# Grouped-query attention with a KV cache: the last two rows of wo re-cut, row 31 in two column halves and row 30 in loads of 120 and 8 partitions

## The chip, the cores and the metric

The kernel runs on one core of a Trainium2 chip. The metric is the device time of one execution in microseconds; lower is better. The kernel before took 363.76 us (median of three runs, 363.58 to 363.94). "Span" is the part of an execution that the profile covers; it is some 1.8 us shorter than the device time. PE is the matrix engine, ACT and DVE are the engines that here cast and copy results, SP is the sequencer that issues the loads (SPq in the views), PEld is PE's loading of weights, and 16 DMA engines move the data. The granted clock is the share of PE's full clock that it had; it was 0.995 to 1.0 in every execution but one (0.99).

## The reference

Shortened:

```python
# B, Sq, D = 32, 4, 1024; Hq, Hkv, Sk, Dh = 32, 4, 2048, 128; all bf16
def reference(x, k_cache, v_cache, wq, wo):
    q = (x @ wq).reshape(B, Sq, Hq, Dh).transpose(0, 2, 1, 3)
    k = jnp.repeat(k_cache, rep, axis=1)          # rep = Hq // Hkv = 8
    v = jnp.repeat(v_cache, rep, axis=1)
    scores = jnp.einsum("bhqd,bhkd->bhqk", q, k) * (Dh ** -0.5)
    p = softmax(scores, axis=-1)
    o = jnp.einsum("bhqk,bhkd->bhqd", p, v)
    return o.transpose(0, 2, 1, 3).reshape(B, Sq, Hq * Dh) @ wo
```

The K and V caches are 134 MB of the 151 MB that are read. wo has 4096 x 1024 elements; the kernel reads it as 32 "rows" (the code's `u` or `h`), each a 128 x 1024 tile of 256 KB, with one matmul contraction of 128 for each row and half of the columns.

## The kernel before: the parts that matter here

SP issues all the loads in one queue: x, wq, then K and V batch by batch, and wo last, into K and V buffers that have come free. The list `WO` says how many rows go into each wo load. The code below is cut out of the kernel; `# ...` marks what is left out.

```python
WO = (4, 4, 4, 4, 4, 4, 2, 2, 2, 1, 1)
# ...
            return big[:, wo_slot[u // 8], :, :].rearrange("p t d -> p (t d)")[:, u % 8 * D:(u % 8 + m) * D]

        wo_v = wo.rearrange("(h p e) n -> p h (e n)", p=128, e=4)
        u0 = 0
        for c, m in enumerate(WO):
            assert u0 // 4 == (u0 + m - 1) // 4
            kind, b = wo_for[u0 // 8]
            dst, src = wo_at(u0, m), wo_v[:, u0 // 4, u0 % 4 * D:(u0 % 4 + m) * D]
            p.dma("sp", lambda e, dst=dst, src=src: e.dma_start(dst, src),
                [("kt", b, 1) if kind == "k" else ("pv", b)], ("wo", c), f"s_wo{c}")
            u0 += m
        assert u0 == Hq
```

The output projection takes the rows in order. Each row is two matmuls of 512 columns, which add to two halves of a PSUM tensor over all rows; a row's matmuls wait for the semaphore of the load that holds the row. Then ACT and DVE cast a half each, and two DMAs write the result.

```python
        def oproj(c):
            for h in range(sum(WO[:c]), sum(WO[:c + 1])):
                for j in range(2):
                    out_, lhsT, rhs = ps_s[:, NC * j:NC * (j + 1)], oT_of(h), wo_at(h, 1)[:, NC * j:NC * (j + 1)]
                    if j == 0:
                        mm = lambda e, a=(out_, lhsT, rhs), h=h: e.matmul(
                            a[0], lhsT=a[1], rhs=a[2], start=(h == 0), stop=(h == Hq - 1), skip_group_check=True)
                    else:
                        mm = lambda e, a=(out_, lhsT, rhs), h=h: _matmul_held(
                            nc, e, *a, tile_size=(128, 128), tile_position=(0, 0), start=(h == 0), stop=(h == Hq - 1))
                    p.op("pe", mm, [("wo", c), ("ot", B - 1)], ("op", j) if h == Hq - 1 else None)

        def oproj_out():
            p.op("act", lambda e: e.activation(y_sb[:, 0:NC], ps_s[:, 0:NC], ACT.Copy), [("op", 0)], ("oe", 0))
            p.op("dve", lambda e: e.tensor_copy(y_sb[:, NC:D], ps_s[:, NC:D]), [("op", 1)], ("oe", 1))
            for j, eng in enumerate(("act", "sp")):
                p.dma(eng, lambda e, j=j: e.dma_start(out_flat[:, NC * j:NC * (j + 1)], y_sb[:, NC * j:NC * (j + 1)]),
                      [("oe", j)], ("out", j), f"s_o{j}")
```

## Time and profile before

| | before |
|---|---|
| device time, median | 363.76 us |
| span of the profiled run | 361.8 us |
| DMA engines | full at about 430 GB/s from the second slice of 40 to the last but one |
| last K or V load complete | 338.15 us |
| rows 28 and 29 (one load) complete | 356.86 us |
| row 30 complete | 357.50 us |
| row 31 complete | 358.13 us |
| last matmul starts | 358.43 us |
| end of the span | 361.8 us |

Two kinds of record are read in this document. The views of the profile (page, chain of waits, timeline, windows) show instructions and waits. Below them, the trace has two lists that no view prints: the time of each semaphore increment by which a DMA engine reports its share of a load, and the start, the duration and the size of each DMA packet. Numbers from these lists stand in plain fences or tables. A load of 128 partitions reports 16 increments; it is complete with the 16th. The packet list has them as packets of 4 bytes: 1296 for the 81 DMAs that SP issues in the kernel before, 16 each. That kernel's packets of the loads from 353 us on chain into 16 strings, each start within 8 ns of the end before it; where a string can be followed, eight packets of a load come before one of 4 bytes. A packet here is one contiguous run: 8 KB for four rows, 4 KB for two, 2 KB for one, 1 KB for half a row.

### The profile page before, as it was taken

How to read it: one execution, taken by the hardware profiler on the slowest of the kernel's cores; microseconds unless marked ns; L12 is line 12 of the kernel's file. 1: busy time of each engine (PE TensorE's matmuls, PEld its weight loads, DVE VectorE, ACT ScalarE, POOL GpSimd, SP SyncE). 2: the span in 40 equal slices, each digit the busy share in tenths (PEclk: the TensorE clock that was granted, in tenths of full speed). 3: DMA queues.
4: the chain of work that ended last, by engine and by line, in shares of the span. 5: the costliest groups of instructions: out<-in, count | busy, mean ns of one | idle time of the engine just before them, and what ended most of it. 6: DMA issues, size and time to landing. Idle time of an engine off the chain costs nothing. (4 is left out here: it accounts for less than half of the span.)

```text
span 361.8 us, 6213 instructions
## 1 busy us (share of the span) xinstructions
PE 307.2 (85%) x3002; PEld 146.8 (41%) x2338; DVE 269.1 (74%) x170; ACT 102.8 (28%) x110; POOL 165.3 (46%) x262
## 2 busy tenths in 40 slices
PE   1988788999989999988999888888888889889896
PEld 1002000454444554444444444444333344449711
DVE  0018799999899888879998888888888888856500
ACT  1014222333333333333333333333322223333000
POOL 8002055355555555554455444445555554444000
PEclk9999999999999999999999999999999999999999
DMA  8999999999999999999999999999999999999995
GB/s 322 431 435 429 431 426 424 431 428 426 423 426 431 426 433 424 430 427 429 431 422 433 428 429 422 431 429 427 431 422 433 429 429 426 427 433 429 408 417 195
DMA packets 11819, 151.66 MB, mean 419 GB/s; under 512 B 1312, under 2 KB 1568, under 8 KB 2336
## 3 DMA queue, kind: packets, MB, share of 16 engines
q1 hardware_dynamic: 11664, 151.39, 98.7%
q8 instruction: 6, 0.10, 0.1%
q10 hardware_dynamic: 144, 0.13, 0.1%
q14 instruction: 5, 0.04, 0.0%
HBM read 151.26 MB, written 0.26 MB: 419 GB/s over the span
## 5 line engine op out<-in xcount | busy, mean ns | idle before, releaser
L325 DVE STREAM_TRANSPOSE KT_sb<-big 128x2048 f32<-128x2048 f32 x64 | 146.6, 2293 | 16.7 <-DMA big<-in_k_cache_dram 16.7
L351 ACT ACTIVATE P_sb<-ps_s,negmx 128x2048 bf16<-128x2048 f32 x32 | 82.1, 2565 | 185.0 <-DVE negmx L347 185.0
L16 PE MATMUL ps_s<-KT_sb,QD_sb 128*128 128x512 bf16 x384 | 103.7, 377 | 0.0
L382 POOL COPY PD_sb<-PT_sb 32x1024 f32<-32x1024 f32 x62 | 64.1, 1034 | 63.4 <-PE ps_r L391 60.5
L382 POOL COPY big<-PT_sb 32x1024 f32<-32x1024 f32 x61 | 63.0, 1034 | 59.1 <-PE ps_r L391 56.4
L347 DVE TENSOR_REDUCE negmx<-ps_s 128x1 f32<-128x2048 f32 x32 | 73.2, 2287 | 12.4 <-PE ps_s L16 11.0
L391 PE MATMUL ps_r<-big 128*128 128x128 bf16 x1024 | 59.8, 219 | 11.3 <-PEq L85 11.3
L391 PE MATMUL ps_r<-big,PD_sb 128*128 128x128 bf16 x1024 | 59.8, 219 | 9.9 <-PEq L85 9.9
L391 PEld LDWEIGHTS ps_r<-big 128*128 128x128 bf16 x1024 | 57.9, 98 | 22.1 <-issue 21.6
L391 PEld LDWEIGHTS ps_r<-big,PD_sb 128*128 128x128 bf16 x1024 | 58.0, 98 | 21.1 <-issue 20.6
L338 PE MATMUL ps_s<-KT_sb,QD_sb 128*128 128x512 bf16 x128 | 48.3, 377 | 18.4 <-PEq L85 18.4
L338 PEld LDWEIGHTS ps_s<-KT_sb,QD_sb 128*128 128x128 bf16 x128 | 12.4, 97 | 103.1 <-issue 103.1
L360 DVE STREAM_TRANSPOSE PT_sb<-P_sb 128x1024 f32<-128x1024 f32 x32 | 39.8, 1245 | 15.8 <-ACT P_sb L351 15.8
L315 POOL COPY QD_sb<-QT_sb 32x64 f32<-32x64 f32 x128 | 29.4, 229 | 46.2 <-DVE QT_sb L294 20.5
L16 PE MATMUL ps_r<-ident 128*128 128x384 bf16 x173 | 33.3, 325 | 0.0
L363 PEld LDWEIGHTS ps_r<-ssum,permf 128*128 128x128 f32 x64 | 11.9, 187 | 24.8 <-issue 23.1
L400 ACT ACTIVATE QT_sb<-ps_r,rinv 128x128 bf16<-128x128 f32 x32 | 11.7, 367 | 29.5 <-PE ps_r L391 27.3
L276 DVE TENSOR_SCALAR KT_sb<-ps_r 128x512 bf16<-128x512 f32 x2 | 1.3, 686 | 20.2 <-PE ps_r L260 20.2
L417 PE MATMUL ps_s<-big,KT_sb 128*128 128x512 bf16 x32 | 12.2, 380 | 2.2 <-DMA big<-in_wo_dram 1.4
L426 DVE CAST P_sb<-ps_s 128x512 bf16<-128x512 f32 x1 | 0.7, 692 | 16.1 <-PE ps_s L16 16.1
L16 PE MATMUL ps_s<-big,KT_sb 128*128 128x512 bf16 x32 | 12.1, 379 | 0.0
L249 PE MATMUL ps_r<-ident 128*128 128x384 bf16 x32 | 10.3, 323 | 0.0
(41 smaller groups left out, 85.1 us busy)
## 6 DMA issues: line engine op xcount, KB each, us to landing
big<-in_k_cache_dram SPq DMA_DIRECT2D x32, 2048.0 KB, 18.6
big<-in_v_cache_dram SPq DMA_DIRECT2D x32, 2048.0 KB, 22.0
big<-in_wq_dram SPq DMA_DIRECT2D x4, 2048.0 KB, 14.1
big<-in_wo_dram SPq DMA_DIRECT2D x6, 1024.0 KB, 22.8
big<-in_wo_dram SPq DMA_DIRECT2D x3, 512.0 KB, 24.5
big<-in_wo_dram SPq DMA_DIRECT2D x2, 256.0 KB, 21.0
P_sb<-in_x_dram SPq DMA_DIRECT2D x1, 256.0 KB, 2.7
out_dram<-P_sb ACTq DMA_DIRECT2D x1, 128.0 KB, 1.8
```

Source lines behind the costliest of these rows:

```text
L16: return eng.add_instruction(mybir.InstMatmult(name=nc.get_next_instruction_name(), engine=eng.engine, start_tensor_calc=start, stop_tenso ...
L315: p.op("pool", lambda e, s=src, d=dst: e.tensor_copy(d, s), waits if g == 0 else [("pt", i - 2)] * (g == 1 and i > 1), ("qd", i) if g == G ...
L325: p.op("dve", lambda e, s=src, d=dst: e.transpose(d, s), waits, ("kt", i, c), gives="t_kt" if c else None)
L338: mm = lambda e, a_=(out_, lhsT, rhs), f=first, l=last: e.matmul(a_[0], lhsT=a_[1], rhs=a_[2], start=f, stop=l, skip_group_check=True)
L347: p.op("dve", lambda e: e.tensor_reduce(negmx[:, i % 4:i % 4 + 1], ps_s[:, :], AX.X, ALU.max, negate=True), [("qk", i)], ("negmx", i))
L351: p.op("act", lambda e: e.activation(P_sb[:, :, :, :].rearrange("p t r w -> p t w r"), ps_s[:, :].rearrange("p (t w r) -> p t w r", w=2, r=R),
L360: p.op("dve", lambda e: e.transpose(dst, src), [("exp", i)], ("pt", i))
L363: p.op("pe", lambda e: e.matmul(ring[(i if i == L else i // 2 * 2) % 4][:, 510 + i % 2:511 + i % 2], lhsT=permf[:, :], rhs=ssum[:, i % 4:i ...
L382: p.op("dve" if i >= B - 2 and g < i - B + 4 else "pool", lambda e, s=src, d=dst: e.tensor_copy(d, s), [free] * (g == 0 or i >= B - 2) + [ ...
L391: p.op("pe", lambda e: e.matmul(buf[:, 0:Dh], lhsT=pd_of(i)[:, t // 2, :, :, :, t % 2].rearrange("p x g q -> p (x g q)"), rhs=big[:, slot_ ...
L400: p.op("act", lambda e: e.activation(dst, src, ACT.Copy, scale=rinv[:, i % 4:i % 4 + 1]), [("pv", i), ("rinv", i)], ("o", i))
L417: mm = lambda e, a=(out_, lhsT, rhs), h=h: e.matmul(a[0], lhsT=a[1], rhs=a[2], start=(h == 0), stop=(h == Hq - 1), skip_group_check=True)
```

## The change

The intent: the last load that lands is complete only when its slowest engine is done (row 31's 15th increment is at 357.96 us, its 16th at 358.13). The change takes row 30's share off one engine (120 partitions go on 15 engines), gives the eight partitions left to eight engines (the changed kernel's packets of 4 bytes are 1319, which is 81 x 16 + 15 + 8), and cuts row 31 into two column halves, so that PE can begin with the first while the second still lands. The matmuls and the output are the same.

```diff
-    NC = D // 2
-    WO = (4, 4, 4, 4, 4, 4, 2, 2, 2, 1, 1)
+    WO = (4, 4, 4, 4, 4, 4, 2, 2, 2, 1)
+    NA = 512
+    COLS = ((0, 0, NA), (NA, NA, D))
     IDLE = 384
     scale = float(Dh) ** -0.5
 
@@ -214,15 +215,18 @@
             return big[:, wo_slot[u // 8], :, :].rearrange("p t d -> p (t d)")[:, u % 8 * D:(u % 8 + m) * D]
 
         wo_v = wo.rearrange("(h p e) n -> p h (e n)", p=128, e=4)
-        u0 = 0
-        for c, m in enumerate(WO):
-            assert u0 // 4 == (u0 + m - 1) // 4
-            kind, b = wo_for[u0 // 8]
-            dst, src = wo_at(u0, m), wo_v[:, u0 // 4, u0 % 4 * D:(u0 % 4 + m) * D]
-            p.dma("sp", lambda e, dst=dst, src=src: e.dma_start(dst, src),
-                [("kt", b, 1) if kind == "k" else ("pv", b)], ("wo", c), f"s_wo{c}")
-            u0 += m
-        assert u0 == Hq
+        pieces = [(sum(WO[:c]), m, 0, D) for c, m in enumerate(WO)] + [(Hq - 1, 1, 0, NA), (Hq - 1, 1, NA, D)]
+        assert sum(WO) == Hq - 1
+        for c, (u, m, n0, n1) in enumerate(pieces):
+            assert u // 4 == (u + m - 1) // 4
+            kind, b = wo_for[u // 8]
+            dst, src = wo_at(u, m), wo_v[:, u // 4, u % 4 * D:(u % 4 + m) * D]
+            if m == 1:
+                dst, src = dst[:, n0:n1], src[:, n0:n1]
+            parts = ((0, 120), (120, 128)) if c == len(pieces) - 3 else ((0, 128),)
+            for i, (p0, p1) in enumerate(parts):
+                p.dma("sp", lambda e, dst=dst[p0:p1], src=src[p0:p1]: e.dma_start(dst, src),
+                    [("kt", b, 1) if kind == "k" else ("pv", b)], ("wo", c, i), f"s_wo{c}_{i}")
# ... (the output projection takes rows one by one, and each matmul waits for the pieces that hold its columns)
+        def oproj(u):
+            for j, (at, n0, n1) in enumerate(COLS):
# ...
+                piece = next(c for c, (v, m, a, z) in enumerate(pieces) if v <= u < v + m and a <= n0 and n1 <= z)
+                p.op("pe", mm, [("wo", piece, i) for i in range(2) if ("wo", piece, i) in p.at] + [("ot", B - 1)], ("op", j) if u == Hq - 1 else None)
```

More of the change, by code (lines that the diff above doesn't have):

```diff
@@ L410, in oT_of @@
             return oT_sb[:, u // 4, u % 4 // 2, :, :, u % 2].rearrange("p b s -> p (b s)")
-        def oproj(c):
-            for h in range(sum(WO[:c]), sum(WO[:c + 1])):
-                for j in range(2):
-                    out_, lhsT, rhs = ps_s[:, NC * j:NC * (j + 1)], oT_of(h), wo_at(h, 1)[:, NC * j:NC * (j + 1)]
-                    if j == 0:
-                        mm = lambda e, a=(out_, lhsT, rhs), h=h: e.matmul(
-                            a[0], lhsT=a[1], rhs=a[2], start=(h == 0), stop=(h == Hq - 1), skip_group_check=True)
-                    else:
-                        mm = lambda e, a=(out_, lhsT, rhs), h=h: _matmul_held(
-                            nc, e, *a, tile_size=(128, 128), tile_position=(0, 0), start=(h == 0), stop=(h == Hq - 1))
-                    p.op("pe", mm, [("wo", c), ("ot", B - 1)], ("op", j) if h == Hq - 1 else None)
+        def oproj(u):
+            for j, (at, n0, n1) in enumerate(COLS):
+                out_, lhsT, rhs = ps_s[:, at:at + n1 - n0], oT_of(u), wo_at(u, 1)[:, n0:n1]
+                if j == 0:
+                    mm = lambda e, a=(out_, lhsT, rhs): e.matmul(
+                        a[0], lhsT=a[1], rhs=a[2], start=(u == 0), stop=(u == Hq - 1), skip_group_check=True)
+                else:
+                    mm = lambda e, a=(out_, lhsT, rhs): _matmul_held(
+                        nc, e, *a, tile_size=(128, 128), tile_position=(0, 0), start=(u == 0), stop=(u == Hq - 1))
+                piece = next(c for c, (v, m, a, z) in enumerate(pieces) if v <= u < v + m and a <= n0 and n1 <= z)
+                p.op("pe", mm, [("wo", piece, i) for i in range(2) if ("wo", piece, i) in p.at] + [("ot", B - 1)], ("op", j) if u == Hq - 1 else None)
@@ L424, in oproj_out @@
         def oproj_out():
-            p.op("act", lambda e: e.activation(y_sb[:, 0:NC], ps_s[:, 0:NC], ACT.Copy), [("op", 0)], ("oe", 0))
-            p.op("dve", lambda e: e.tensor_copy(y_sb[:, NC:D], ps_s[:, NC:D]), [("op", 1)], ("oe", 1))
-            for j, eng in enumerate(("act", "sp")):
-                p.dma(eng, lambda e, j=j: e.dma_start(out_flat[:, NC * j:NC * (j + 1)], y_sb[:, NC * j:NC * (j + 1)]),
+            p.op("act", lambda e: e.activation(y_sb[:, 0:NA], ps_s[:, 0:NA], ACT.Copy), [("op", 0)], ("oe", 0))
@@ L429, in oproj_out @@
+            p.op("dve", lambda e: e.tensor_copy(y_sb[:, NA:D], ps_s[:, NA:D]), [("op", 1)], ("oe", 1))
+            for j, (eng, n0, n1) in enumerate((("act", 0, NA), ("sp", NA, D))):
+                p.dma(eng, lambda e, n0=n0, n1=n1: e.dma_start(out_flat[:, n0:n1], y_sb[:, n0:n1]),
                       [("oe", j)], ("out", j), f"s_o{j}")
@@ L474, in bass_standalone__gqa_block_cached__sampling_kernel @@
             o_turn(b0, n)
-        for c in range(len(WO)):
-            oproj(c)
+        for u in range(Hq):
+            oproj(u)
         oproj_out()
```

## The prediction

> **What bounds the kernel now.** I read the page first, for the bound of the whole run. Its second part gives DMA and the bytes moved in 40 slices of about 9 us.
>
> ```profile
> DMA  8999999999999999999999999999999999999995
> GB/s 322 431 435 429 431 426 424 431 428 426 423 426 431 426 433 424 430 427 429 431 422 433 428 429 422 431 429 427 431 422 433 429 429 426 427 433 429 408 417 195
> ```
>
> The 16 DMA engines are full, at some 430 GB/s, from the second slice to the last but one. The change touches none of that: it re-cuts only the last two of the 32 rows of wo (a row is 128 x 1024 bf16, 256 KB), at the very end of the queue. So the question is what sets the last few microseconds. For that I read the chain of waits in order of time (start, length, what).
>
> ```profile
> 330.84 1.14 SPq L222
> 331.98 0.38 issue
> 332.36 24.50 DMA big<-in_wo_dram
> 356.86 0.05 issue
> 356.91 0.39 PE ps_s L417
> 357.30 0.21 PE ps_s L16
> 357.52 0.22 PE ps_s L417
> 357.73 0.22 PE ps_s L16
> 357.95 0.22 PE ps_s L417
> 358.16 0.22 PE ps_s L16
> 358.38 0.22 PE ps_s L417
> 358.60 0.23 PE ps_s L16
> 358.82 0.02 issue
> 358.85 0.69 DVE P_sb L426
> ```
>
> The chain comes out of one DMA at 356.86 and then is on PE for eight matmuls without a pause. Eight matmuls are four rows: so the DMA is the last load of TWO rows (28 and 29, the third of the 512 KB issues), not the load of row 30 or of row 31. The timeline of the same stretch (start, length, instruction, idle before it and what ended that) confirms it.
>
> ```profile
> 356.91 0.39 PE L417 MATMUL ps_s<-big,KT_sb 128*128 128x512 bf16 x1 [0.18 <-DMA big<-in_wo_dram]
> ...
> 358.18 0.10 PEld L417 LDWEIGHTS ps_s<-big,KT_sb 128*128 128x128 bf16 x1 [0.51 <-DMA big<-in_wo_dram]
> 358.22 0.38 PE L417 MATMUL ps_s<-big,KT_sb 128*128 128x512 bf16 x1
> 358.43 0.38 PE L16 MATMUL ps_s<-big,KT_sb 128*128 128x512 bf16 x1
> 358.63 0.60 ACT L425 ACTIVATE P_sb<-ps_s 128x512 bf16<-128x512 f32 x1 [16.21 <-PE ps_s L417]
> 358.85 0.69 DVE L426 CAST P_sb<-ps_s 128x512 bf16<-128x512 f32 x1 [16.09 <-PE ps_s L16]
> ```
>
> Only the first matmul of row 28 has idle PE before it. Row 31's weight load did wait for row 31's DMA, until 358.18, but its matmul began at 358.22, which is when PE was due anyway: the matmul before it began at 358.00, and matmuls follow each other every 0.216 us here. After the last matmul come a cast (0.69 us), the issue of the output and its landing: the span ends 3.0 us after 358.85.
>
> The trace also records each of a load's 16 semaphore increments (one per DMA engine). For the last three loads, us from the span's start:
>
> ```
> rows 28+29  first 354.82  15th 356.69  16th 356.86
> row 30      first 355.50  15th 357.33  16th 357.50
> row 31      first 356.16  15th 357.96  16th 358.13
> ```
>
> Two things are to be seen. One engine is always last, by 0.17 to 0.18 us. And row 31, complete at 358.13, is about level with PE: its slack is some 0.04 us. So there are two limits at the same place: PE's string of eight matmuls from 356.91, and row 31's landing.
>
> [...] The trace of the kernel before has only loads of 128 partitions; their 16 increments each agree, and no load in it shows a smaller number. [...] the trace shows one last engine but not its number. [...] the last two wo issues took 2.1 us on SP, and the wo loads 20.3 to 24.8 us from issue to landing.
>
> **The change part by part.** The cost of packets comes from the trace's packet records near the end: a 2048-byte packet follows another on the same engine after 0.080 us, and the increments of rows 30 and 31 lie 0.635 us apart on the last engine, or 0.646 us by the starts of its increment packets, which is eight packets of 0.080 plus 0.006 for the increment. A 1024-byte packet is recorded at 0.046 us against 0.084, so I take 0.042 for its step.
>
> 1. Row 30 in 120 + 8 partitions. [...]
>
> 2. Row 31 in two halves. Each engine carries eight packets of 1 KB twice: 2 x (8 x 0.042 + 0.006) = 0.68 us where it was 0.65, so the second half lands +0.04 us late and the first half 0.34 us before the second.
>
> 3. Sum for row 31's second half. [...] The first half is there 0.34 earlier: 357.66 to 357.92.
>
> 4. When PE needs them. With rows 28 and 29 complete at 356.86 as before (their load is the same, and lies ahead of all that changes in every ring), row 30's first matmul is due at 357.79, row 31's first at 358.22, and its second, which now waits for the second half alone, at 358.43. Row 30 is complete at 357.50 + 0.09 = 357.59 at the latest, row 31's first half at 357.92, the second at 358.26. From an increment to PE's start takes 0.05 us (356.86 to 356.91). All three are there in time. So the last matmul begins at 358.43 as before, and the sum on the path is **0.00 us**. What the change does win is slack: the second half is wanted 0.21 us after the first, so row 31's slack grows from 0.04 us to between 0.12 and 0.38. That is worth nothing while the two-row load holds PE.
>
> 5. Added instructions. SP gets two more issues (66 rows for 64). At 2.1 us each, as measured for the last two, the last issue would end near 344 instead of 339.98, 12 us before its packets start: hidden. PE gets two more waits (row 30's second semaphore, the second half's). They are handled while PE works off a string at 0.216 us each; I put them at 0 to 0.05 us. Matmuls, casts and output are the same in number, size and order.
>
> **The rivals.**
>
> (a) Row 31's landing is the true end, and relieving the last engine brings it forward. For it: the wait at 358.18, and that the two limits are level. Against it: PE had no idle time before row 31's matmul, and 28 and 29's load, which holds the string, is untouched. Even if right, PE cannot start row 31 before 358.22, so the gain is that slack of 0.04 us at most: 363.7.
>
> (b) The added load makes a new wait. [...] the 120-partition load is spread over the partitions less well and its packets take longer than 0.080 us. For it: nothing in the trace shows a load of 120. Against it: row 30 has 0.15 us to spare and the second half 0.12 even with the last engine hit; packets would have to be a fifth slower. It would make 0.1 to 0.3 us: 363.9 to 364.1.
>
> (c) The extra waits or a shift of the instruction stream stall PE's string. PE is the bound exactly there, so each 0.05 us counts in full: 363.8 to 363.9.
>
> (d) The whole stream gets faster because the slow engine is relieved. Against it: [...] the increments' spread was already 2.0 us at 83 us and stayed so, so the slow engine paces the whole stream, and the change comes after it. At most nothing.
>
> **Range and chances.** The step sum is 0.00, (a) gives -0.04, (b) and (c) +0.05 to +0.3. Three runs of the kernel before spread over 0.36 us, more than any of these. I predict **363.76 us**, range **363.4 to 364.15**. Two per cent is 7.3 us, and all that follows the landing of rows 28 and 29 at 356.86 is 5.0 us of the span: within 2% has 0.985, faster 0.005, slower 0.01.
>
> **What would show it right or wrong.** In the changed kernel's chain of waits there should again be one DMA of wo followed by eight matmuls in a string, with the DMA's end at 356.8 to 356.9 and the cast's start at 358.8 to 358.9. In the timeline no PE idle before row 31's matmuls, and no wait of its second matmul. In the increments: row 30's 120 partitions with 15 increments, row 31's second half last by less than the 0.17 of before if the relieved engine was the slow one. Wrong would be: the string starting earlier than 356.8 (then the load of rows 28 and 29 depends on what comes behind it), a pause in the string, or a chain whose DMA is now the half or the eight-partition load.

The times in parts 3 and 4 are estimates of mine from the numbers of the kernel before. A row's 128 packets with 16 increments make eight packets to an engine, so I counted 15 engines for 120 partitions and one relieved of its 0.65 us. For the other eight partitions I assumed eight engines, with one packet and one increment more each (0.080 + 0.006 = 0.09 us). Which engines these are no trace of the kernel before shows. If the last engine is the one relieved, row 31's second half lands with the engine that was 15th, at 357.96 + 0.04 = 358.00; if the last engine gets the extra packet, it lands at 358.13 + 0.09 + 0.04 = 358.26.

## The result

The changed kernel took **364.16 us** (median of four runs, 364.03 to 364.52) against 363.67 us of the kernel before in the same rounds (363.33 to 363.94). The ratio is 1.0017, with a 95% interval of 1.0002 to 1.0032. Ratios in this document are from fast runs of the same rounds. In the experiments they come out as ratios of means with the first run of each list left out, so they are not quite the ratio of the medians that are quoted beside them; for the pair here means give 1.0016 with all runs and 1.0018 without the first. So the change costs about half a microsecond. That is "the same" by a threshold of 2%, and it lies just above my range of 363.4 to 364.15.

The chain of waits of the changed kernel (start, length, what), to be held against the one in the prediction:

```profile
332.29 25.16 DMA big<-in_wo_dram
357.45 0.05 issue
357.50 0.39 PE ps_s L420
...
359.19 0.23 PE ps_s L16
359.42 0.02 issue
359.44 0.69 DVE P_sb L430
```

It has the shape that I predicted, one DMA of wo and then eight matmuls. But the DMA ends at 357.45 instead of 356.86, and all that follows is 0.59 us later. The span grew by 0.60 (361.84 to 362.44). The timeline shows which load it is:

```profile
356.62 0.38 PE L16 MATMUL ps_s<-big,KT_sb 128*128 128x512 bf16 x1
357.50 0.33 PEld L420 LDWEIGHTS ps_s<-big,KT_sb 128*128 128x128 bf16 x2 [1.21 <-DMA big<-in_wo_dram]
357.50 0.39 PE L420 MATMUL ps_s<-big,KT_sb 128*128 128x512 bf16 x1 [0.50 <-DMA big<-in_wo_dram]
...
358.81 0.38 PE L420 MATMUL ps_s<-big,KT_sb 128*128 128x512 bf16 x1
359.02 0.38 PE L16 MATMUL ps_s<-big,KT_sb 128*128 128x512 bf16 x1
```

The matmul that waits is row 28's. There is no pause in the string behind it, and row 31's two matmuls start back to back. So the late load is that of rows 28 and 29, which the change doesn't touch and which lies ahead of all that it touches.

The windows view says when it came about. Its columns are the window, its length, busy time (and number) for PE, PEld, DVE, ACT and POOL, then the granted clock, the DMA share and GB/s. First the kernel before, then the changed one:

```profile
353.00:354.50 1.50, 1.40 (x7) 0.39 (x4) 0.00 (x0) 0.00 (x0) 0.00 (x0) 1.00 1.01 400
354.50:355.50 1.00, 1.00 (x7) 0.20 (x2) 0.00 (x0) 0.00 (x0) 0.00 (x0) 1.00 1.04 404
356.50:357.50 1.00, 0.82 (x5) 0.20 (x2) 0.00 (x0) 0.00 (x0) 0.00 (x0) 1.00 0.37 141
```

```profile
353.00:354.50 1.50, 1.50 (x8) 0.36 (x5) 0.00 (x0) 0.00 (x0) 0.00 (x0) 1.00 1.03 410
354.50:355.50 1.00, 0.95 (x5) 0.18 (x2) 0.00 (x0) 0.00 (x0) 0.00 (x0) 1.00 1.07 291
356.50:357.50 1.00, 0.50 (x3) 0.00 (x1) 0.00 (x0) 0.00 (x0) 0.00 (x0) 1.00 0.62 202
```

Up to 354.5 the two are alike. Between 354.5 and 355.5, when the fast engines have reached row 30 (their first 2-KB packet starts at 354.29) and the slow ones still work at rows 26 to 29, the engines are as busy as before (1.04 and 1.07) and move 291 GB/s instead of 404. The packets themselves take longer. From the trace's packet list, the mean duration in us of the packets that start in each half microsecond, with the longest in brackets:

| packets starting in | before, 2 KB | before, 4 KB | changed, 2 KB | changed, 4 KB |
|---|---|---|---|---|
| 354.0 to 354.5 | 0.085 (0.087) | 0.164 (0.172) | 0.085 (0.087) | 0.164 (0.172) |
| 354.5 to 355.0 | 0.085 (0.094) | 0.164 (0.172) | 0.112 (0.174) | 0.220 (0.312) |
| 355.0 to 355.5 | 0.087 (0.096) | 0.163 (0.172) | 0.147 (0.166) | 0.245 (0.292) |

The 4-KB packets belong to the loads that the change left alone. They take up to 0.312 us, 1.96 times 0.159, the most frequent duration of a 4-KB packet in the kernel before.

The increments of the last loads of the changed kernel (us from the span's start):

```
rows 28+29    first 354.79  15th 357.37  16th 357.45
row 30, 120   one at 337.92 (the issue), then 355.90 355.94 355.95 355.97 ... 357.98 358.02
row 30, 8     one at 339.74 (the issue), then 356.26 ... 358.08 358.21
row 31 a      first 355.96, second 356.20      16th 358.40
row 31 b      first 356.35                     16th 358.61
```

### The profile page after: what moved, and what is told of

Same layout as the page of the kernel before. It is cut to its first block, busy times and chain, and to the rows that moved or that the text cites. A ratio compares the mean times of both kernels' runs of the same rounds, so it can differ in the third digit from the quotient of the medians.

```text
span 362.4 us, 6212 instructions
## 1 busy us (share of the span) xinstructions
PE 307.3 (85%) x2998; PEld 146.8 (41%) x2338; DVE 269.1 (74%) x170; ACT 102.7 (28%) x110; POOL 165.3 (46%) x262
## 5 line engine op out<-in xcount | busy, mean ns | idle before, releaser
L367 PEld LDWEIGHTS ps_r<-ssum,permf 128*128 128x128 f32 x64 | 11.9, 187 | 24.8 <-issue 23.1
L16 PE MATMUL ps_s<-big,KT_sb 128*128 128x512 bf16 x32 | 12.1, 379 | 1.2 <-DVE KT_sb L411 1.1
L420 PE MATMUL ps_s<-big,KT_sb 128*128 128x512 bf16 x30 | 11.4, 381 | 1.9 <-DMA big<-in_wo_dram 1.9
```

The source lines that it names most:

```text
L16: return eng.add_instruction(mybir.InstMatmult(name=nc.get_next_instruction_name(), engine=eng.engine, start_tensor_calc=start, stop_tenso ...
L367: p.op("pe", lambda e: e.matmul(ring[(i if i == L else i // 2 * 2) % 4][:, 510 + i % 2:511 + i % 2], lhsT=permf[:, :], rhs=ssum[:, i % 4:i ...
L420: mm = lambda e, a=(out_, lhsT, rhs): e.matmul(a[0], lhsT=a[1], rhs=a[2], start=(u == 0), stop=(u == Hq - 1), skip_group_check=True)
```

## The experiments

Three theories stood after the first reading. (A) The load of 120 partitions makes DMA engines collide, so that packets slow down, on loads ahead too. (B) The small 1-KB packets of the halves do it. (C) The load of eight partitions does it, since eight engines (its eight increments) then write to eight neighbouring partitions. Twelve runs were made, three of which time kernels of this document again. Each diff is against the changed kernel unless another is named. The first table sums up what the single changes gave; "4 KB, longest" is the longest packet of the two-row loads, and the load of rows 28 and 29 is complete where the last column says.

| run | row 30 | row 31 | time, us | 4 KB, longest | rows 28+29 complete |
|---|---|---|---|---|---|
| before (first profile) | 128 | whole | 363.76 | 0.172 | 356.86 |
| changed (first profile) | 120 + 8 | halves | 364.16 | 0.312 | 357.45 |
| e1_halves_only | 128 | halves | 363.41 | 0.172 | 356.62 |
| e2_split_only | 120 + 8 | whole | 364.13 | 0.286 | 357.22 |
| e3_120_alone | 120 | whole | 364.06, one run | 0.322 | 357.29 |
| e4_8_beside | 128, and 8 more | whole | 363.61, one run | 0.175 | 356.80 |
| e5_window_0_64 | 64 (0 to 63) | 64 | 364.49, one run | 0.316 | 357.70 |
| e6_window_32_96 | 64 (32 to 95) | 64 | 363.82, one run | 0.172 | 357.04 |

One more reading does not depend on how far a whole stream is shifted in a run: the time in us from the last increment of rows 24 and 25 to the last of rows 28 and 29. Rows 24 to 29 are three loads of two rows, which every run but e7, e8 and f4 issues alike.

```
before 2.53   e1 2.54   e4 2.55   e6 2.51   f3 2.56      (no load of 120 partitions or of 0 to 63)
changed 3.26  e2 3.14   e3 3.25   f1 3.32   f2 3.32      (row 30 in 120 partitions)
e5 3.43                                                  (rows 30 and 31 in partitions 0 to 63)
```

The first four of the e runs were on one chip, the next four on another. In the first group's rounds the kernel before had a median of 363.83 us with a wide spread (363.28 to 365.18, and one slow run of 639 us that counts for nothing), so the traces and not the times decide there; the times were measured again below. In the second group's rounds before had a median of 363.43 us.

### Halves alone

```diff
-            parts = ((0, 120), (120, 128)) if c == len(pieces) - 3 else ((0, 128),)
+            parts = ((0, 128),)
```

> Row 30 in one load of 128 partitions, row 31 in two halves. Theory A (the 120-partition load makes engines share destinations, so that packets of rows 28 and 29 on the slow engines are stretched): no stretched packets here, 4-KB packets stay at 0.16 us and below 0.18, rows 28+29 complete at 356.86 as before, time within 0.15 us of before. Theory B (the 1-KB packets of the halves are what disturbs): the 4-KB packets of rows 28+29 stretch up to 0.3 us as in the change, that load completes some 0.5 us late, time +0.4 to +0.6. Theory C (the eight-partition load does it): as A here.

Measured: 363.41 us, ratio 0.9995 (0.9959 to 1.0031). Its chain:

```profile
332.13 24.48 DMA big<-in_wo_dram
356.62 0.05 issue
356.66 0.39 PE ps_s L420
```

No packet of 4 KB takes more than 0.172 us, and the window 354.5 to 355.5 moves 401 GB/s. Theory B is out: 1-KB packets are harmless here. The load is complete at 356.62, a little earlier than in the profile of before: the slowest engine trails the 15th by 0.07 us here and by 0.17 there, and the 15th is itself 0.15 us earlier (356.54 for 356.69). Both vary from run to run.

### The split alone

```diff
-        pieces = [(sum(WO[:c]), m, 0, D) for c, m in enumerate(WO)] + [(Hq - 1, 1, 0, NA), (Hq - 1, 1, NA, D)]
+        pieces = [(sum(WO[:c]), m, 0, D) for c, m in enumerate(WO)] + [(Hq - 1, 1, 0, D)]
-            parts = ((0, 120), (120, 128)) if c == len(pieces) - 3 else ((0, 128),)
+            parts = ((0, 120), (120, 128)) if c == len(pieces) - 2 else ((0, 128),)
```

> Row 30 in 120 + 8 partitions, row 31 whole. Theories A and C: rows 28+29 complete at about 357.45 instead of 356.86, 4-KB packets up to 0.3 us, and the time is +0.4 to +0.6 over before, as in the whole change. Theory B: as before, within 0.15.

Measured: 364.13 us, ratio 1.0004 (0.9977 to 1.0031), which the spread of before makes useless. The chain and the window between 354.5 and 355.5 decide:

```profile
357.22 0.05 issue
357.26 0.39 PE ps_s L420
```

```profile
354.50:355.50 1.00, 0.95 (x5) 0.10 (x1) 0.00 (x0) 0.00 (x0) 0.00 (x0) 1.00 1.08 315
```

315 GB/s, 4-KB packets up to 0.286 us, rows 28 and 29 complete at 357.22. The split carries the stretch by itself.

### 120 partitions without the eight

Against the split alone:

```diff
-            parts = ((0, 120), (120, 128)) if c == len(pieces) - 2 else ((0, 128),)
+            parts = ((0, 120),) if c == len(pieces) - 2 else ((0, 128),)
```

> As the split alone, but the eight last partitions of row 30 are not loaded at all: a wrong result, on purpose. Theory A: still the stretch, 4-KB packets to about 0.3 us, rows 28+29 complete at 357.2 to 357.5. Theory C: no stretch, complete at 356.86. Either way the engine that carries nothing of row 30 shows itself: the load of row 31 has one increment early by some 0.65 us against its rank; I expect it among the first six, not the last.

Measured: wrong, as row 30's last eight partitions keep old data; 364.06 us in the one run. 4-KB packets up to 0.322 us, rows 28 and 29 complete at 357.29. So the eight-partition load isn't needed for the stretch: theory C is out as its sole cause. The engine that carries nothing of row 30 shows itself as well. Row 31's first increment comes at 355.98, and the earliest of row 30's at 355.65. A whole row takes 0.65 us on an undisturbed engine (0.635 between the last increments of rows 30 and 31 in the kernel before), so the engine of 355.98 has not carried row 30. It finished rows 28 and 29 some 0.65 earlier, at about 355.3, and the increments of that load up to 355.93 are six: 354.69 to 355.14. The engine left out is one of the first six, not the last.

### Eight partitions beside a whole row

```diff
+            if c == len(pieces) - 2:
+                p.dma("sp", lambda e, src=src: e.dma_start(P_flat[120:128, 0:D], src[120:128]), [("pt", B - 1)], "extra8", "s_extra8")
```

(on top of rows 30 and 31 whole; the end of the kernel waits for it)

> Rows 30 and 31 whole, as before, and an extra load of eight partitions of row 30 behind row 30, into a dead part of the P buffer. Theory A: little or no stretch, 4-KB packets below 0.2 us but for the few that meet the eight; rows 28+29 complete within 0.1 of 356.86. Theory C: the full stretch, 4-KB packets up to 0.3 us and rows 28+29 complete near 357.4.

Measured: correct, 363.61 us in the one run, 4-KB packets at most 0.175 us, rows 28 and 29 complete at 356.80. The load of eight alone stretches nothing that matters. It also tells where the slowest engine is: the eight increments of the extra load follow row 30's by 0.19 to 0.24 us when they are matched in order of time (the list does not name engines), and the last of them is at 357.65, 0.22 behind row 30's last at 357.43. So the slowest engine is one of the eight that carry the eight-partition load.

### Two windows of 64 partitions

These two runs take the number of engines out of the question. Rows 30 and 31 load only 64 of their partitions (wrong on purpose), in both cases with 16 increments and 64 packets for a row, four to an increment. Theory A has three readings here: engines get in each other's way by the partitions that they write (A1), by being 15 or by uneven shares (A2), or on the HBM side (A3). The diff is against the kernel with rows 30 and 31 whole.

```diff
-            parts = ((0, 128),)
+            parts = ((0, 64),) if c >= len(pieces) - 2 else ((0, 128),)
```

> Rows 30 and 31 load only partitions 0 to 63, on all 16 engines with four partitions each: a wrong result, on purpose. [...] Theory A1[...]: the 2-KB packets stretch to about 0.16 us, and the 4-KB packets of rows 28+29 on slow engines stretch too, although all 16 engines carry the same. Theory A2 (it is the 15 engines or the uneven shares as such): no stretch, 0.084. Theory A3 (the stretch is on the HBM side, from the order of the rows read): the same as with the other window of 64 partitions.

The other run has `((32, 96),)` in the same place.

> As the run before, but partitions 32 to 95: same packets, same shares, same pattern of rows read, another window. [...] Theory A1: no stretch, 2-KB packets 0.084 us, 4-KB packets below 0.18. A2: as the other window, no stretch in either. A3: as the other window, stretch in both or in neither.

Measured, the chain and the window 354.5 to 355.5 of partitions 0 to 63:

```profile
357.70 0.05 issue
357.74 0.39 PE ps_s L420
```

```profile
354.50:355.50 1.00, 1.00 (x7) 0.20 (x2) 0.00 (x0) 0.00 (x0) 0.00 (x0) 1.00 0.95 252
```

and of partitions 32 to 95:

```profile
357.04 0.05 issue
357.08 0.39 PE ps_s L420
```

```profile
354.50:355.50 1.00, 1.00 (x7) 0.20 (x2) 0.00 (x0) 0.00 (x0) 0.00 (x0) 1.00 0.85 334
```

The GB/s are lower than before's in both, as the rows are half as large and engines run out of work (DMA shares 0.95 and 0.85), so the packets are the comparison. In the half microsecond from 355.0, with partitions 0 to 63 the 2-KB packets take 0.161 us in the mean and the 4-KB ones of rows 26 to 29 take 0.304; with partitions 32 to 95 they take 0.085 and 0.163. The stretch is there or not there by the choice of the 64 partitions alone, with the same number of engines, packets and bytes, and where it is there it is a factor of 1.9. This is what theory A1 forecast, and here it needs neither 15 engines nor uneven shares. What makes the first window slower than the second, and which engine writes which of the 64 partitions, no record shows. The run with 32 to 95 is 0.39 us above the median of before, and no stretched packet goes with that: its slowest engine trails the 15th by 0.37 us already in rows 24 and 25, before the window loads. One more reservation: the rows of HBM that are read shift with the window, by the same 32 rows, though their order and spacing are the same. No run moved only the one side, so a cause on the HBM side is made unlikely, not excluded.

### The same cut on a load four times as large

Against the kernel with rows 30 and 31 whole (`c == 5` is the load of rows 20 to 23):

```diff
-            parts = ((0, 128),)
+            parts = ((0, 120), (120, 128)) if c == 5 else ((0, 128),)
```

> The 120 + 8 cut moved to a load four times as large, rows 20 to 23 (1 MB, 8-KB packets), with rows 30 and 31 whole. Theory A1: [...] 8-KB packets up to 0.6 us instead of 0.31, and the cost grows with the bytes: at half rate 1 MB takes 2.4 us longer, so +1.2 to +2.4 us. A fixed cost of a load on an odd number of engines: +0.6 us as in the change. No cost away from the end of the stream: as before.

Measured: 369.16 us (367.29 to 369.30, four runs), ratio 1.0139 (1.0113 to 1.0165), +5.7 us by the medians. The direction and the growth with the bytes are as expected, the size is not: I had expected 1.2 to 2.4. Two things make it up. The 8-KB packets go up to 0.69 us, a little over twice the 0.31 of an undisturbed one, but the stretch hits the 1 MB ahead too (complete at 352.44 instead of 350.56) and the 4-KB packets behind (up to 0.446): rows 20 to 23 are complete at 357.43 instead of 353.06, 4.4 us late. And PE, which waits 2.40 us for them, runs slower:

```profile
357.57 0.59 PE L420 MATMUL ps_s<-big,KT_sb 128*128 128x512 bf16 x1 [2.40 <-DMA big<-in_wo_dram]
357.94 0.63 PE L16 MATMUL ps_s<-big,KT_sb 128*128 128x512 bf16 x1
358.37 0.63 PE L420 MATMUL ps_s<-big,KT_sb 128*128 128x512 bf16 x1
```

The matmuls that start from 357.94 to 359.65 take 0.63 us each and come every 0.43 us; from 360.40 on they take 0.38 and come every 0.22. The 0.63 us were there before the wait too, from 353.68 to 354.53. The mean granted clock of this profiled run was 0.99, where it was 0.999 or 1.0 in the other profiles; why PE slowed is not shown. Behind the landing it costs 6 x 0.21 = 1.3 us more, since the 24 matmuls of twelve rows now stand in one string behind that landing.

### Single rows, with and without the halves

With PE held by the string behind the two-row load, a version that takes the string away should beat both kernels: rows 28 and 29 each in a load of its own.

```diff
-    WO = (4, 4, 4, 4, 4, 4, 2, 2, 2, 1)
+    WO = (4, 4, 4, 4, 4, 4, 2, 2, 1, 1, 1)
-            parts = ((0, 120), (120, 128)) if c == len(pieces) - 3 else ((0, 128),)
+            parts = ((0, 128),)
```

> A version that should beat both: rows 28, 29 and 30 each in a load of its own with 128 partitions, row 31 in two halves. PE's string of eight matmuls behind the two-row load is gone; the end is then held by row 31's second half, which lands at 358.15 to 358.2 in a run like the profile of before, so that the last matmul starts near 358.25 instead of 358.43. Theory A expects no stretch and a time 0.1 to 0.3 us below before. If the string was not the bound, the time is that of before.

Measured: 363.28 us (363.24 to 363.53, five runs) against 363.43 of before in the same rounds, ratio 0.9994 (0.9980 to 1.0008). The interval includes 1, so it is not shown to be faster than before. The timeline has what was wanted:

```profile
357.85 0.38 PE L420 MATMUL ps_s<-big,KT_sb 128*128 128x512 bf16 x1
358.06 0.38 PE L16 MATMUL ps_s<-big,KT_sb 128*128 128x512 bf16 x1
```

Row 31's second half is complete at 358.02, and the last matmul starts 0.04 us later, at 358.06. In the kernel before it started 0.30 us after the last landing (358.13 to 358.43). So this cut takes away some 0.26 us of what lies between the last landing and the last matmul, and that is about the size of the variation from run to run. It could not take away more: PE itself was due only at 358.06, the fourth of the matmuls that follow row 30's landing at 357.36.

The fourth kernel of the last group has single rows and no halves (f4_ones_whole: `WO = (4, 4, 4, 4, 4, 4, 2, 2, 1, 1, 1)`, row 31 whole).

> Rows 28 to 31 in four loads of one whole row each: the single rows without the halves. If the string and row 31's landing are level, as the profile of before says, taking the string away alone wins next to nothing: -0.05 to 0 us, against -0.15 for single rows with halves (measured on another chip).

Measured: 363.51 us, ratio 1.0008 (0.9992 to 1.0024), no gain. Its last landing is at 358.28 and its last matmul some 0.27 behind: without the halves PE waits for all of row 31 and then has two matmuls to do. Only the two steps together close that distance; that they pay in time is not shown, for either chip.

### Times again, on one chip

The whole change, the split alone and the halves alone, five rounds each, are the kernels of the runs above.

> The changed kernel once more, with the split alone and the halves alone on one chip, for ratios that may be compared. [...] ratio to before 1.0010 to 1.0025 (+0.4 to +0.9 us), rows 28+29 complete 0.4 to 0.7 us later than in the profile of the halves alone.

> Row 30 in 120 + 8, row 31 whole. [...] the same as the whole change within 0.2 us, since all of its cost is here.

> Row 30 whole, row 31 in halves. My string argument (PE is held by eight matmuls behind rows 28+29): 0.00 from before, within 0.15 us. If the halves win by themselves (the other limit, row 31's landing, was the real one): -0.1 to -0.2 us.

| kernel | median, us | ratio to before | 95% interval | rows 28+29 complete |
|---|---|---|---|---|
| before | 363.39 | | | |
| whole change | 364.28 | 1.0019 | 1.0006 to 1.0032 | 357.83 |
| split alone | 364.29 | 1.0024 | 1.0012 to 1.0036 | 357.79 |
| halves alone | 363.56 | 1.0001 | 0.9988 to 1.0013 | 356.82 |

The whole change and the split alone are 0.9 us slower by the medians and 0.01 us apart. The halves alone are within the noise of before. The load of rows 28 and 29 comes 1.0 us later with the split than without it in these profiles, more than the 0.4 to 0.7 that I had expected (0.6 in the first pair). Some 0.25 us of it is not the split: rows 24 and 25 were complete that much later already (354.52 and 354.47 against 354.27). Counted from there the delay is 0.76 us, and 0.73 in the first pair.

## Why the prediction was wrong

It gave 363.76 us with a range up to 364.15; 364.16 was measured, and 364.28 in the second group. The sign, not only the last hundredth, was missed: I had summed the path to 0.00, and it is +0.5 to +0.9.

**The step that failed** is in part 4: "With rows 28 and 29 complete at 356.86 as before (their load is the same, and lies ahead of all that changes in every ring)". The premise agrees with the trace (a "ring" here is the string of packets of one DMA engine, and in the kernel before each increment of rows 28 and 29 comes 0.63 to 0.69 us ahead of row 30's of the same rank), and the conclusion does not follow from it. Being ahead in each ring says that an engine does not have to finish row 30 before rows 28 and 29. It says nothing about what another engine does to it. The fast engines are 2 us ahead of the slow ones (in the kernel before, the increments of one load spread over 0.5 us in the loads complete between 8 and 53 us of the span, and over 2.0 to 2.2 us from 74 us to the last wo load), so they were writing row 30 while the slow ones still wrote rows 26 to 29, and in the 120-partition cut the packets of both were slower: 2-KB packets took 0.147 us in the mean from 355.0 on instead of 0.087, 4-KB packets took up to 0.312 us instead of 0.16, and the load was complete at 357.45. The spread of 2 us was in my own table of increments; I used it for the last engine only and did not ask who writes where meanwhile.

**The mechanism**, as far as it is shown: which partitions a small load covers decides whether the engines get in each other's way, by a factor of 1.9 (the two windows: 2-KB packets 0.161 us with partitions 0 to 63, 0.085 with 32 to 95, on 16 increments each). What the engines share there is not shown. That the 120-partition load is slow for the same reason is an inference from the like size of the stretch (4-KB packets up to 0.312 us there, up to 0.316 with partitions 0 to 63). No record here shows which engine wrote which partition.

**The other steps.**

- Part 1, the relieved engine: the case in which the last engine is the one relieved was wrong. It was a guess: the trace of the kernel before shows one last engine, not which engine a smaller load leaves out. In the runs, the engine without row 30 is among the first six (done with rows 28 and 29 by 355.14 us in e3, the last at 357.29), and the slowest is one of those that got the eight partitions besides (e4). So the cut relieves an engine that had time to spare and adds a packet to the one that had none. Even without the slower packets it would not have helped.
- Part 2, the halves: right within 0.05 us. With halves alone the second half completes 0.65 us after row 30 (357.27 to 357.92), against an estimate of 0.68, and the first 0.29 before it, against 0.34.
- Part 4, the need of PE: right. There is one string of eight matmuls behind rows 28 and 29 with no pause in it, before and after, and the halves won nothing while it stood. With the string cut to four, the last matmul follows the last landing by 0.04 us instead of 0.30.
- Part 5: right. The last wo issue ended at 344.2 us (predicted near 344), and the string of the changed kernel takes 357.50 to 359.02, 1.52 us, exactly as before (356.91 to 358.43), so the added waits of PE cost nothing.
- Rival (b) came nearest in one clause ("the 120-partition load is spread over the partitions less well and its packets take longer") and put it in the wrong place: I applied it to row 30 and row 31's slack, where it would have cost 0.1 to 0.3, and not to the load ahead, which had no slack. Rivals (a), (c) and (d) did not happen.
- "What would show it right or wrong" asked for the DMA's end at 356.8 to 356.9, and it was at 357.45. As a sign that rows 28 and 29 depend on what comes behind them it named only the string starting earlier than 356.8, and not later.
- Three readings on the way were off and changed nothing. The 20.3 to 24.8 us from issue to landing are those of the last five wo loads, not of all. SP issues 81 DMAs before and 83 after, not 64 and 66. And the first packet of row 31 started at 354.73 in the changed kernel, 10.5 us after the last issue ended, not 12.

## What to carry to other kernels

When a load is cut into pieces, ask not only how many engines carry a piece but which partitions they write while their neighbours are still at the load before: a piece that was meant to relieve one engine can slow others, and with them a load that lies ahead (here 4-KB packets of up to 0.312 us instead of 0.172, and the load ahead complete 0.59 us later). Before you relieve "the slowest engine", find out which one it is; a small extra load (e4), or a load with one engine left out (e3), shows something of it in the increments. And where two limits are level, taking one away need not win anything: here only single rows and halves together brought the last matmul up to the last landing, and even that was within the noise.
